# An adaLN block with attention and feed-forward, forward and backward: how the first head group is placed, who normalises, and where chunk 0's side work stands

## The chip, the cores and the metric

The kernel runs on one core of a Trainium2 chip. The metric is device time in microseconds (us), less is better. Five engines work beside each other, each through its own instructions in order: PE (matmul), DVE (VectorE), ACT (ScalarE), POOL (GpSimd) and SP, which here only issues DMAs.

## The reference, cut to what matters

The output is the block's forward value and, through `jax.vjp`, the gradients of nine inputs. Only the forward matters below; the gradients need w_mod, wqkv, w1, w2 and wo transposed too.

```python
mod = (_silu(c) @ w_mod).reshape(c.shape[0], 6, 1, -1)
sa, ca, ga, sb, cb, gb = ...
h = _layernorm(x, axis=-1) * (1 + ca) + sa
# S = 2048 tokens, D = 512, H = 32 heads of Dh = 16
q, k, v = (h @ wqkv) in heads
p = _softmax(einsum('bhqd,bhkd->bhqk', q, k) * Dh ** (-0.5))
x = x + ga * (einsum('bhqk,bhkd->bhqd', p, v) @ wo)
h = _layernorm(x, axis=-1) * (1 + cb) + sb
x = x + gb * ((relu(h @ w1 + b1) ** 2) @ w2 + b2)
```

## The kernel before

**Stages.** `prep` (L824) normalises all tokens, transposes them to h1T, projects the keys of heads 0 to 7 for all tokens and the queries of the first 512, and finds a bound for the scores. Then the forward loop (L1113) runs over 512 units: 4 query chunks of 512 tokens, 8 head groups of 4 heads, 16 key tiles of 128. A unit computes scores for four heads (`fscore`, L544), exponentiates them on ACT in two instructions (L555), and multiplies the values for the unit two before (`fpv`, L557). After a chunk its dense work (projection, feed-forward and their gradients) runs in the next chunk's units. The attention's backward comes last; the change does not touch it.

**The bound.** Instead of a row maximum the softmax subtracts -|q| max|k|. It is carried inside the score matmul: each head's 32 rows of `kts` and `qts` hold 16 rows of keys or queries, one row of ones against one row of the bound, and unused rows. In `prep`, head group 0's rows are put there by small DMAs from the projected tile (`key_rows`, L867, sixteen of them; four for the queries; one for the bound at the end). The other groups are loaded by `fload` (L537) from DRAM, nine DMAs each: four for keys, four for queries, one for the bound (`m_st`). It is issued six units before the group's first unit, into the one of two buffers that is free.

**Order of prep.** For each quarter g of the tokens: statistics on DVE (`stats_tiles`), square root on ACT (`stats_root`), normalisation (`normed1`, L756: two tiles on POOL, two on DVE), PE transposes (`turn1`, L765), four ACT instructions that scale and shift (L775), key projection, its evacuation by ACT (L906). `keep_warm` issues matmuls whose result is not used. At the end come key maxima (L786), square root (L926), the bound row and the first four value tiles.

**Chunk 0's side work.** While units 0 to 127 run, three lists are worked off. `plan_tasks` (L943) puts one task into most units: value tiles, key and query projections for the other heads (`key_tile`, `query_tile`), norms (`key_norm`), bounds (`query_bound`, a DVE chain spread over units), rows of the modulation (`mod_rows`), and PE transposes of queries and keys into token order (`token_tile`). All of them share one PSUM buffer (`pm`, one bank). `later_stage` (L652) runs one stage every fourth unit, at u % 4 = 2: weights and values transposed by DMA into DRAM scratch (stages 4 to 13 and 0 to 3), w_mod transposed (26 to 31: four DMA transposes and a store each), and the normalised tokens recomputed and stored (14 to 25; L692 to L694 are their DVE work). `turn_weights` (L702) transposes w1, w2 and wo by DMA at u % 4 = 0.

**Queues.** Inside `manual_schedule` each engine keeps the written order. Every DMA through `sp` (L173) and `load_rows` (L138) is on SP's queue: a DMA that has to wait for its source holds back all DMAs behind it. `later(lag, ...)` emits an instruction `lag` units later.

## Time and profile before

| what | value |
|---|---|
| runs | median of 13: 2607.01 us, 2602.54 to 2622.65 us |
| the profiled execution | 2605.89 us, of which the span is 2604.1 us |
| busy over the span | PE 90%, ACT 88%, DVE 69%, POOL 14% |
| prep, to the first score matmul | 0 to 48.65 us |
| chunk 0, first exponential to first of chunk 1 | 49.1 to 315.7 us |
| two exponentials of one unit, where nothing stalls | 1.81 us |
| chunks 1 to 3 | 315.7 to about 1065 us |
| attention backward and the end | the rest |

Times in rows of the profile are microseconds from the start of the span. A row of the timeline gives start, duration, engine, line, operation, `output<-input`, shapes, and in square brackets how long the engine had been idle and what ended that. `PEclk` is the share of full clock that PE was granted. SPq stands for DMAs being issued on SP.

### The profile page before, as it was taken

To read this page: it belongs to the slowest core of one execution; us is meant where nothing else is said; L and a number is where in the kernel's file an instruction comes from. 1 tells how busy PE (TensorE), PEld (TensorE's weight loads), DVE (VectorE), ACT (ScalarE), POOL (GpSimd) and SP (SyncE) were. 2 spreads that over 40 slices of the span, in tenths; PEclk is the share of its full clock that TensorE was granted. 3 is DMA by queue.
4 is the path that set the end of the run, shared out by engine and by line. 5 is a ranking of instruction groups with operands and counts; after the bars stand their busy time and mean duration, and the time that the engine had idled before them with its cause. 6 is when DMAs were issued, how large, how long until landed. Compare 5 with 4: busy or idle time off the path is not lost.

```text
span 2604.1 us, 49454 instructions
## 1 busy us (share of the span) xinstructions
PE 2351.6 (90%) x18444; PEld 760.7 (29%) x18444; DVE 1808.6 (69%) x2301; ACT 2303.5 (88%) x3565; POOL 363.6 (14%) x371
## 2 busy tenths in 40 slices
PE   7995989988988889898999999999999999999999
PEld 3232123222322222342222222222232222222343
DVE  5551354445344534578999999999998999999862
ACT  5995999999999999737999999999999999999942
POOL 4000010211233123201110101111011110110100
PEclk8885569997989899999999999999999999999999
DMA  3556565346847673989999999999999999999982
GB/s 128 156 152 169 169 142 135 99 124 136 140 88 139 135 136 77 237 250 195 199 190 199 197 200 193 190 203 197 195 199 198 205 191 197 190 198 206 197 249 73
DMA packets 1227775, 447.49 MB, mean 172 GB/s; under 512 B 1103419, under 2 KB 1198399, under 8 KB 1227278
## 3 DMA queue, kind: packets, MB, share of 16 engines
q1 hardware_dynamic: 1199614, 409.47, 79.8%
q0 software_dynamic: 10944, 16.78, 4.5%
q10 hardware_dynamic: 16976, 18.07, 2.5%
q8 instruction: 145, 2.38, 0.4%
q14 instruction: 96, 0.79, 0.1%
HBM read 96.75 MB, written 73.95 MB: 66 GB/s over the span
## 4 chain that ended last, share of the span: by engine, by line
PE 47%; ACT 34%; DVE 7%; issue 6%; DMA 3%; SPq 2%; POOL 1%; ACTq 0%; DVEq 0%; POOLq 0%
ACT E_u L1552 21%; ACT ET L555 9%; PE dqacc L1624 6%; PE psST L553 5%; PE psS_A L1546 4%; ACT dsT L1695 3%; PE accVK L1597 3%; PE pm L228 3%; PE oacc L569 3%; PE psS_C L1546 2%; PE psS_B L1546 2%; PE pm L393 2%; PE accVK L1606 2%; PE pdh L1810 2%; PE pwq L1844 2%
## 5 line engine op out<-in xcount | busy, mean ns | idle before, releaser
L1566 DVE TENSOR_TENSOR dS_u<-psD_u,E_u 128x1024 bf16<-128x1024 f32 x1024 | 1186.5, 1216 | 99.7 <-PE psS_B L1546 41.0
L555 ACT ACTIVATE ET<-psST 128x1024 bf16<-128x1024 f32 x1024 | 946.3, 1180 | 72.6 <-PE psST L553 72.0
L1552 ACT ACTIVATE E_u<-psS_A 128x512 bf16<-128x512 f32 x768 | 508.8, 663 | 20.0 <-PE psD_u L1564 9.0
L1552 ACT ACTIVATE E_u<-psS_B 128x512 bf16<-128x512 f32 x768 | 504.5, 657 | 3.9 <-PE psS_A L1546 0.5
L1564 PE MATMUL psD_u<-iv,ido 32*128 32x512 bf16 x2048 | 423.0, 397 | 0.2
L553 PE MATMUL psST<-qt_sb,kt_sb 32*128 32x512 bf16 x2048 | 356.9, 439 | 64.8 <-ACT ET L555 33.8
L1552 ACT ACTIVATE E_u<-psS_C 128x512 bf16<-128x512 f32 x512 | 335.0, 654 | 2.3 <-DMA dsT<-dS_u 1.8
L1546 PE MATMUL psS_B<-ik,iq 32*128 32x512 bf16 x768 | 305.4, 398 | 10.3 <-ACT E_u L1552 2.8
L1546 PE MATMUL psS_A<-ik,iq 32*128 32x512 bf16 x768 | 303.3, 395 | 12.5 <-ACT E_u L1552 1.3
L569 PE MATMUL oacc<-ET,vaug 128*32 128x512 bf16 x2048 | 235.1, 449 | 5.7 <-DVE ostage L573 5.7
L1597 PE MATMUL accVK<-dS_u,qz 128*32 128x512 bf16 x2048 | 226.1, 411 | 0.3 <-DVE dS_u L1566 0.2
L1546 PE MATMUL psS_C<-ik,iq 32*128 32x512 bf16 x512 | 194.0, 379 | 33.8 <-ACT dsT L1695 29.8
L1546 PEld LDWEIGHTS <-iq 32*128 32x128 bf16 x2048 | 128.3, 91 | 308.7 <-issue 293.5
L1606 PE MATMUL accVK<-E_u,dOs_tok 128*16 128x512 bf16 x2048 | 209.1, 398 | 0.0
L1642 POOL TENSOR_TENSOR dQacc<-dQacc,dqtmp 128x512 f32<-128x512 f32 x64 | 81.2, 1268 | 870.3 <-ACT dqtmp L1637 870.3
L1624 PE MATMUL dqacc<-dsT,KS_tok 128*32 128x512 bf16 x2048 | 181.1, 462 | 15.1 <-DMA dsT<-dS_u 4.2
L553 PEld LDWEIGHTS <-kt_sb 32*128 32x128 bf16 x2048 | 86.6, 93 | 357.6 <-issue 322.2
L246 DVE COPY part<-pm 128x512 f32<-128x512 f32 (+2 forms) x103 | 63.5, 616 | 132.2 <-PE pm L228 130.3
L1695 ACT ACTIVATE dsT<-ptT 128x1024 bf16<-128x1024 bf16 x128 | 149.0, 1164 | 3.0 <-PE ptT L1587 3.0
L1564 PEld LDWEIGHTS <-ido 32*128 32x128 bf16 x2048 | 106.8, 91 | 106.2 <-issue 100.8
L1597 PEld LDWEIGHTS <-qz 128*32 128x32 bf16 x2048 | 61.0, 98 | 241.2 <-issue 228.0
L1587 PE MATMUL ptT<-identb,dS_u 128*128 128x128 bf16 x1024 | 79.8, 222 | 32.9 <-ACT dsT L1695 26.0
(389 smaller groups left out, 2315.3 us busy)
## 6 DMA issues: line engine op xcount, KB each, us to landing
p_st<-part POOLq DMA_DIRECT2D x36, 256.0 KB, 5.3
kt_sb<-qkT_st SPq DMA_DIRECT2D x124, 64.0 KB
wA<-in_B_w_dram SPq DMA_DIRECT2D x28, 256.0 KB
dsT<-dS_u SPq DMA_TRANSPOSE x448
wB<-w1T_st SPq DMA_DIRECT2D x21, 256.0 KB
wA<-w2T_st SPq DMA_DIRECT2D x21, 256.0 KB
wB<-in_B_w_dram SPq DMA_DIRECT2D x21, 256.0 KB
p_st<-part POOLq DMA_DIRECT2D x25, 192.0 KB, 4.4
```

Source lines behind the costliest of these rows:

```text
L553: PE.matmul(ps[:, hi, :], kt_sb[r:r + 32, kt * P:(kt + 1) * P], qt_sb[r:r + 32, :], start=True, stop=True, tile_position=(r, 0))
L555: ACT.activation(ET[:, 2 * pair:2 * pair + 2, :], ps[:], AF.Exp, scale=SCALE)
L569: PE.matmul(oacc[32 * hq:32 * hq + 32, :], lhsT, ET[:, hq, :], start=(kt == 0), stop=(kt == TT - 1), tile_position=(0, 32 * hq), skip_grou ...
L1546: PE.matmul(psS[:], st["q"][r:r + 32, qt * P:(qt + 1) * P], st["k"][r:r + 32, kc * 512:kc * 512 + 512], start=True, stop=True, tile_positi ...
L1552: ACT.activation(bst[u][0][:, hq, :], sst.pop((u, hq))[:], AF.Exp, scale=SCALE)
L1564: PE.matmul(psD[:, hi, :], st["do"][r:r + 32, qt * P:(qt + 1) * P], st["v"][r:r + 32, kc * 512:kc * 512 + 512], start=True, stop=True, til ...
L1566: DVE.tensor_tensor(dS_u[:, 2 * pair:2 * pair + 2, :], psD[:], E_u[:, 2 * pair:2 * pair + 2, :], ALU.mult)
L1597: PE.matmul(cur["vk"][32 * hq:32 * hq + 32, :], hst[hg]["qz"][:, qt, hq, :], bst[u][1][:, hq, :], start=(qt == 0), stop=False, tile_positi ...
L1606: PE.matmul(acc[32 * hq:32 * hq + DH, :], dOs_tok[:, qt, (hg * 4 + hq) * DH:(hg * 4 + hq + 1) * DH], E_u[:, hq, :], start=False, stop=(qt ...
L1624: PE.matmul(acc[32 * hq:32 * hq + 32, :], KS_tok[:, kc * 4 + kt, h * DH:h * DH + 32], tT[:, :, hq * 4 + kt, :], start=(kt == 0), stop=(kt ...
L1642: POOL.tensor_tensor(dst2, dst, tmp[:], ALU.add)
L1695: ACT.activation(dst, pt[:], AF.Identity)
```

## The change

It has five parts. (1) Head group 0's keys, queries and bounds are no longer moved by DMA. The weight columns of four heads are copied into zero-padded tiles (`wkp`, `wqp`: 32 columns for a head, 16 of them filled), a second product with these lands the keys at their 32-row places, and ACT writes them into `kts[0]`, adding the row of ones as a bias (`onecol`). The norms of these heads are summed by a selector `sel0` that lands them in the bound's row and its neighbour, and one DVE instruction over 128 rows writes query rows and bound row into `qts[0]`. (2) `normed1` uses DVE and ACT, two tiles each, not POOL, and group 0 is normalised before the modulation columns are computed. (3) Four of the six w_mod turns (16 DMA transposes, 4 stores) are issued in `prep`, ahead of the loop; stages 26 to 29 leave the loop, the stages behind them come 16 units earlier, and `turn_weights` 4 units later. (4) Chunk 0's tasks are interleaved: projections alternate with norms or transposes. The norms of keys 0 to 7 are computed once more in units 43 to 49. (5) `mod_rows` and the loads of w_mod's second half move from units 23 to 31 to units 51 to 58.

```diff
@@ -723,9 +723,13 @@
         sbcT = small[:, 0:512].rearrange("p (i q) -> p i q", i=DC)
         sel = small[:, 512:640].rearrange("p (b h) -> p b h", b=4)
         siluc_col, c_col = small[:, 640:644], small[:, 644:648]
-        smallf = small[:, 704:1024].bitcast(F32)
+        smallf = small[:, 704:884].bitcast(F32)
+        nb1 = racc[:, 4, 0:TT]
         sig_col, mv, sd, sel8 = smallf[:, 0:4], smallf[:, 4:36].rearrange("p (t k) -> p t k", k=2), smallf[:, 36:52], smallf[:, 52:60]
         kmx, kmax, epsc = smallf[0:H, 64:80], smallf[0:H, 80:81], smallf[:, 81:82]
+        onecol, kmx0, kmax0 = smallf[:, 82:83], smallf[:, 84:88], smallf[:, 88:89]
+        sel0 = small[:, 888:1016]
+        wkp, wqp = (small[:, i:i + 512].rearrange("p (i h c) -> p i h c", i=DC, h=4) for i in (1024, 1536))
         wmod_v = w_mod.rearrange("(ic p) j -> p ic j", p=P)
         wqkv_v = A_wqkv.rearrange("(ic p) j -> p ic j", p=P)
         xcs, xns, h1Ts, KTs = {}, {}, {}, {}
@@ -757,10 +761,14 @@
             gs = slice(4 * g, 4 * g + 4)
             DVE.reciprocal(rstd1[:, gs], sd[:, gs])
             xns[g] = xn = cb.tile([P, 4, D], BF, name="xnP", tag=("a_c", "xn2_c")[g % 2])
-            for ti in (1, 3, 0, 2):
+            gs1 = slice(4 * g, 4 * g + 4)
+            DVE.scalar_tensor_tensor(out=nb1[:, gs1], in0=mv[:, gs1, 0], scalar=-1.0, in1=rstd1[:, gs1], op0=ALU.mult, op1=ALU.mult)
+            for ti in range(4):
                 t = 4 * g + ti
-                (POOL, DVE)[ti % 2 == 0].tensor_scalar(xn[:, ti, :], xcs[g][:, ti, :], mean1[:, t:t + 1], rstd1[:, t:t + 1],
-                                                       ALU.subtract, ALU.mult)
+                if ti % 2:
+                    ACT.activation(xn[:, ti, :], xcs[g][:, ti, :], AF.Identity, bias=nb1[:, t:t + 1], scale=rstd1[:, t:t + 1])
+                else:
+                    DVE.tensor_scalar(xn[:, ti, :], xcs[g][:, ti, :], mv[:, t, 0:1], rstd1[:, t:t + 1], ALU.subtract, ALU.mult)
 
         def turn1(g):
             h1Ts[g] = h1T = (sP[:, 0:4, :] if g == 3 else cb.tile([P, DC, 512], BF, name="h1T", tag=htags[g])[:])
@@ -847,11 +855,17 @@
             ACT.activation(tiny0[:], onesf[:, 0:1], AF.Sqrt)
             DVE.memset(epsc, EPS)
             DVE.memset(kmx, 0.0)
-            DVE.memset(kts[0][:], 1.0)
-            DVE.memset(qts[0][:], 0.0)
             DVE.tensor_reduce(sel8, identb.rearrange("p (i d) -> p i d", d=DH), AX.X, ALU.add)
             DVE.tensor_tensor(siluc_col, c_col, sig_col, ALU.mult)
             DVE.tensor_copy(sbcT, siluc_col.unsqueeze(2).to_broadcast([P, DC, P]))
+            DVE.tensor_reduce(onecol, identb.rearrange("p (h c) -> p c h", c=32)[:, DH, :], AX.X, ALU.add)
+            POOL.memset(sel0, 0.0)
+            POOL.memset(wkp, 0.0)
+            POOL.memset(wqp, 0.0)
+            for k in range(2):
+                POOL.tensor_copy(sel0.rearrange("p (h c) -> p c h", c=32)[:, DH + k, :], sel8[:, 4 * k:4 * k + 4])
+            POOL.tensor_copy(wkp[:, :, :, 0:DH], wqkv[:, :, D:D + 4 * DH].rearrange("p i (h d) -> p i h d", h=4))
+            POOL.tensor_copy(wqp[:, :, :, 0:DH], wqkv[:, :, 0:4 * DH].rearrange("p i (h d) -> p i h d", h=4))
             POOL.memset(sel, 0.0)
             for b in range(4):
                 POOL.tensor_copy(sel[:, b, 8 * b:8 * b + 8], sel8)
@@ -864,34 +878,48 @@
                 for _ in range(k):
                     PE.matmul(warm[:], ones_bf[:], identb.unsqueeze(1).to_broadcast([P, 4, P]), start=True, stop=True)
 
-            def key_rows(g):
-                for h in range(4):
-                    sp(kts[0][32 * h:32 * h + DH, chunk_cols(g)], KTs[0][DH * h:DH * h + DH, chunk_cols(g)])
-
             def acc4():
                 return psp["p"].tile([P, 512], F32, name="pk", tag="pk", bufs=3)
 
             sq = tmpT[:, 8:13, :]
             pns = {}
 
-            def norms(i, b=0):
-                pns[i] = psp["p"].tile([P, 512], F32, name="pn", tag="pn", bufs=1) if i < 4 else \
-                    psp["p"].tile([P, 512], F32, name="pnq", tag="pcol", bufs=1)
-                head_norms(pns[i], sq[:, i, :], b)
-
+            def norms(i):
+                pns[i] = psp["p"].tile([P, 512], F32, name="pn", tag="pn" if i < 4 else "pcol", bufs=1)
+                PE.matmul(pns[i][:], sel0, sq[:, i, :], start=True, stop=True)
+
+            def widest(g):
+                DVE.tensor_reduce(kmx0[:, g:g + 1], pns[g][:], AX.X, ALU.max)
+
+            def padded_proj(acc, w, g):
+                for ic in range(DC):
+                    PE.matmul(acc, w[:, ic].rearrange("p h c -> p (h c)"), h1Ts[g][:, ic, :], start=(ic == 0), stop=(ic == DC - 1))
+
+            def wmod_turn(j):
+                for q in range(4):
+                    sp(tmpT[:, 4 * (j % 2) + q, :], w_mod[:, (4 * j + q) * P:(4 * j + q + 1) * P], True)
+                if j > 0:
+                    wmod_store(j - 1)
+
+            def wmod_store(j):
+                sp(wmT_st[j], tmpT[:, 4 * (j % 2):4 * (j % 2) + 4, :])
+
+            for j in range(4):
+                wmod_turn(j)
+            wmod_store(3)
             stats_tiles(0, range(4))
             stats_root(0)
             keep_warm(16)
+            stats_tiles(1, (0,))
+            normed1(0)
             mod_cols_of(psp["p"].tile([P, 8], F32, name="pcol", tag="pcol", bufs=1), 0, 2)
             keep_warm(4)
-            normed1(0)
-            stats_tiles(1, (0,))
             for g in range(QC):
                 if g < 3:
                     stats_tiles(g + 1, (1, 2, 3))
                 turn1(g)
                 if g > 1:
-                    key_max(pns[g - 2], 0, g - 2)
+                    widest(g - 2)
                 if g < 2:
                     stats_tiles(g + 2, (0,))
                 if g < 3:
@@ -904,31 +932,35 @@
                 pk = acc4()
                 turned_proj(pk[:], 1, g, 0)
                 ACT.activation(KTs[0][:, chunk_cols(g)], pk[:], AF.Identity)
-                key_rows(g)
+                pk = acc4()
+                padded_proj(pk[:], wkp, g)
+                ACT.activation(kts[0][:, chunk_cols(g)], pk[:], AF.Identity, bias=onecol)
                 if g > 0:
                     norms(g - 1)
-                if g == 2:
+                if g == 1:
                     pq = acc4()
                     turned_proj(pq[:], 0, 0, 0)
                     ACT.activation(sP[:, 4, :], pq[:], AF.Identity)
-                    for h in range(4):
-                        sp(qts[0][32 * h:32 * h + DH, :], sP[DH * h:DH * h + DH, 4, :])
+                if g == 2:
                     square(sq[:, 4, :], sP[:, 4, :])
                     norms(4)
             sp(qkT_st[1, 0:P, :], KTs[0][:])
             sp(qkT_st[0, 0:P, 0:512], sP[:, 4, :])
-            key_max(pns[2], 0, 2)
+            widest(2)
             square(sq[:, 3, :], KTs[0][:, chunk_cols(3)])
             norms(3)
-            key_max(pns[3], 0, 3)
-            DVE.tensor_reduce(kmax, kmx, AX.X, ALU.max)
+            pq = acc4()
+            padded_proj(pq[:], wqp, 0)
+            widest(3)
+            DVE.tensor_reduce(kmax0, kmx0, AX.X, ALU.max)
             qn = cb.tile([P, 512], F32, name="qn", tag="part", bufs=4)
-            ACT.activation(qn[0:H, :], pns[4][0:H, :], AF.Sqrt, scale=kmax)
+            ACT.activation(qn[:], pns[4][:], AF.Sqrt, scale=kmax0)
             ACT.activation(tiny0[:], onesf[:, 0:1], AF.Exp)
-            mrow = sP[0:H, 13, :]
-            DVE.tensor_scalar(mrow, qn[0:H, :], -1.0, None, ALU.mult)
-            sp(qts[0].rearrange("(h c) n -> c h n", h=4)[DH], mrow[0:4, :])
-            sp(m_st[0:8, 0:512], mrow[0:8, :])
+            DVE.scalar_tensor_tensor(out=qts[0][:], in0=qn[:], scalar=-1.0, in1=pq[:], op0=ALU.mult, op1=ALU.add)
+            mrow = sP[:, 13, :]
+            DVE.tensor_scalar(mrow, qn[:], -1.0, None, ALU.mult)
+            for k in range(2):
+                sp(m_st[4 * k:4 * k + 4, 0:512], mrow.rearrange("(h c) n -> c h n", h=4)[DH + k])
             for t in range(4):
                 value_tile(t, acc4()[:])
             POOL.memset(kts[1][:], 1.0)
@@ -982,8 +1014,7 @@
                     head_norms(pn, T["q"][:, hb, :], hb, hb == hbs[0], hb == hbs[-1])
                 for k in "vyt":
                     R[k] = cb.tile([P, 512], F32, name="rt" + k, tag="part", bufs=4)[0:H, :]
-                if hbs[0] != 0:
-                    DVE.tensor_reduce(kmax, kmx, AX.X, ALU.max)
+                DVE.tensor_reduce(kmax, kmx, AX.X, ALU.max)
                 DVE.tensor_scalar(R["v"], pn[0:H, :], kmax, 1e-30, ALU.mult, ALU.max)
 
             def bound(g, hbs):
@@ -1036,35 +1067,37 @@
 
             for t in range(4, TT):
                 at(t - 4, lambda t=t: value_tile(t, mm()[:]))
+            for b, units in ((1, (12, 13, 15, 17)), (2, (23, 24, 26, 28)), (3, (32, 35, 37, 39))):
+                for g, u in enumerate(units):
+                    at(u, key_tile, b, g)
+            for b, units in ((0, (43, 45, 47, 49)), (1, (14, 16, 18, 20)), (2, (25, 27, 29, 31)), (3, (34, 36, 38, 40))):
+                for g, u in enumerate(units):
+                    if b == 0:
+                        at(u - 1, lambda g=g: square(T["k"][:, g, :], KTs[0][:, chunk_cols(g)]))
+                    at(u, key_norm, b, g)
+            for hb, u in ((1, 19), (2, 30), (3, 33)):
+                at(u, query_tile, 0, hb)
             for g in range(QC):
-                at(12 + g, key_tile, 1, g)
-                at(17 + g, key_norm, 1, g)
-                at(26 + g, key_tile, 2, g)
-                at(31 + g, key_norm, 2, g)
-                at(35 + g, key_tile, 3, g)
-                at(40 + g, key_norm, 3, g)
-                at(45 + g, query_tile, 1, g)
-                at(49 + g, token_tile, 0, 0, g)
-                at(54 + g, query_tile, 2, g)
-                at(58 + g, token_tile, 0, 1, g)
-                at(63 + g, query_tile, 3, g)
-                at(72 + g, token_tile, 0, 2, g)
-                at(76 + g, token_tile, 0, 3, g)
+                at(42 + 2 * g, query_tile, 1, g)
+                at(58 + 2 * g, query_tile, 2, g)
+                at(73 + 2 * g, query_tile, 3, g)
+                at(52 + 2 * g - (g == 3), token_tile, 0, 0, g)
+                at(59 + 2 * g, token_tile, 0, 1, g)
+                at((69, 71, 74, 76)[g], token_tile, 0, 2, g)
+                at(81 + g, token_tile, 0, 3, g)
                 for ti in range(4):
-                    at(80 + 4 * g + ti, token_tile, 1, g, ti)
-            for hb, u in ((1, 16), (2, 30), (3, 39)):
-                at(u, query_tile, 0, hb)
+                    at(85 + 4 * g + ti, token_tile, 1, g, ti)
             query_bound(21, 0, (1,), 2)
             at(22, b1_turn)
+            query_bound(41, 0, (2, 3), 1)
+            query_bound(50, 1, (0, 1, 2, 3), 1)
+            query_bound(66, 2, (0, 1, 2, 3), 1)
+            query_bound(80, 3, (0, 1, 2, 3), 1)
             for j in range(3):
-                at(23 + j, mod_rows, j)
-                at(27 + 2 * j, lambda j=j + 3: sp(wmod_slice(j), wmod_v[:, :, j * D:(j + 1) * D]))
-                at(68 + j, mod_rows, j + 3)
+                at(51 + 2 * j, mod_rows, j)
+                at(56 + j, lambda j=j + 3: sp(wmod_slice(j), wmod_v[:, :, j * D:(j + 1) * D]))
+                at(68 + 2 * j, mod_rows, j + 3)
             at(67, lambda: mod_cols_of(mm(), 3, 2))
-            query_bound(44, 0, (2, 3), 1)
-            query_bound(53, 1, (0, 1, 2, 3), 1)
-            query_bound(62, 2, (0, 1, 2, 3), 1)
-            query_bound(71, 3, (0, 1, 2, 3), 1)
 
         NF = len(funits)
 
@@ -1101,7 +1134,7 @@
             with tc.manual_schedule(engines={PE.engine, ACT.engine, DVE.engine, SP.engine, POOL.engine}):
                 prep()
         plan_tasks()
-        stages = [*range(4, 14), *range(4), *range(26, 32), *range(14, 26)]
+        stages = [*range(4, 14), *range(4), 30, 31, *range(14, 26)]
         with ExitStack() as ph2:
             pools["s"] = ph2.enter_context(tc.tile_pool(name="psS", bufs=3, space=bass.MemoryType.PSUM))
             pools["o"] = ph2.enter_context(tc.tile_pool(name="psO", bufs=1, space=bass.MemoryType.PSUM))
@@ -1117,10 +1150,10 @@
                         fscore(u)
                     if 2 <= u:
                         fpv(u - 2)
-                    if u % 4 == 2 and u // 4 < 32:
+                    if u % 4 == 2 and u // 4 < len(stages):
                         later_stage(stages[u // 4])
-                    if u % 4 == 0 and 17 <= u // 4 < 31:
-                        turn_weights(u // 4 - 17)
+                    if u % 4 == 0 and 18 <= u // 4 < 32:
+                        turn_weights(u // 4 - 18)
                     for f, args in plan.pop(u, ()):
                         f(*args)
                     if u < NF - 4:
```

## The prediction

> **What bounds it now.** First the busy time by stretches, since the change touches only prep and chunk 0.
>
> ```profile
> core 0: us, PE busy (x) PEld busy (x) DVE busy (x) ACT busy (x) POOL busy (x), PEclk, DMA share, GB/s
> 0.00:49.00 49.00, 33.66 (x178) 14.81 (x179) 28.94 (x75) 20.63 (x33) 27.46 (x33) 0.83 0.41 133
> 49.00:171.00 122.00, 113.00 (x713) 33.97 (x710) 66.24 (x121) 116.56 (x127) 5.54 (x9) 0.87 0.54 151
> 171.00:199.00 28.00, 26.23 (x212) 9.73 (x210) 16.53 (x33) 28.00 (x32) 0.61 (x1) 0.86 0.60 157
> 199.00:258.00 59.00, 31.65 (x214) 11.48 (x212) 8.24 (x19) 32.82 (x37) 0.61 (x1) 0.50 0.61 153
> 258.00:316.00 58.00, 53.77 (x256) 10.03 (x252) 23.40 (x28) 58.00 (x65) 1.46 (x2) 0.50 0.67 201
> ```
>
> In prep no engine is full: it is a chain. In chunk 0 ACT is the bound wherever nothing stalls (28.00 of 28.00, 58.00 of 58.00): 128 units of 1.815 us are 232.3 us, and chunk 0 takes 266.6 (49.1 to 315.7). So 34.3 us are stalls, and the waits in that stretch say the same:
>
> ```profile
> ACT ET L555 <- PE psST L553: 34.4, 12, 8.8
> PE psST L553 <- DMA qt_sb<-m_st: 17.3, 2, 9.1
> DVE tokP L1028 <- DMA k_st<-tokP: 7.8, 1, 7.8
> DVE tokP L1028 <- DMA q_st<-tokP: 6.7, 1, 6.7
> ```
>
> Taking the starts of the exponentials unit by unit from the timeline, the excess stands at unit 79 (9.2 us), 89 (4.6), 93 (5.5), 95 (8.0), together 27.3, and at 21 to 24, 35, 45, 62 (7.3). The first four are SP's queue: at 79 and 95 the scores wait for a head group's last load, at 89 and 93 the token tiles wait for a store that frees their buffer. SP in that place:
>
> ```profile
> 196.67 5.44 SPq L173 DMA_TRANSPOSE tmpT<-in_w_mod_dram  x4
> 203.72 0.34 SPq L173 DMA_DIRECT2D wmT_st<-tmpT  x1
> 204.16 2.13 SPq L138 DMA_DIRECT2D kt_sb<-qkT_st  x4
> 206.34 1.80 SPq L138 DMA_DIRECT2D qt_sb<-qkT_st  x4
> 208.18 0.56 SPq L138 DMA_DIRECT2D qt_sb<-m_st  x1
> 210.05 0.71 PE L553 MATMUL psST<-qt_sb,kt_sb 32*128 32x512 bf16 x4 [9.11 <-DMA qt_sb<-m_st]
> ```
>
> The reader is to see: a DMA transpose holds SP 1.3 us, a load 0.46; the store waits for its transposes, and the nine loads stand behind it.
>
> **Part 3, w_mod turns out of the loop.** SP's account for units 58 to 95 (38 units, 69.0 us). Before: 24 w_mod transposes, 14 of w1, 2 of the output, 40 x 1.3 = 52.0; 8 small row DMAs x 0.63 = 5.0; three head loads x 4.3 = 12.9; some 18 others x 0.5 = 9.0; waits of wmT stores 6 x 1.5 = 9.0. Sum 87.9, so 18.9 over. After: 16 transposes go (-20.8), 4 stores and their waits (-8.0): 59.1, which fits. Order matters too, so I follow the queue. Group 5's loads (unit 74) have only x loads, row DMAs and one output transpose ahead of them and land some 4 us before unit 80; the token stores stand at least 4 units ahead of their reuse. Units 79, 89 and 93 lose their 19.3 us. Group 6: from unit 80 SP has 12 w1 transposes (15.6), row DMAs and output transpose (3.8), five stores (2.5), then nine loads (4.2), landing about 2 us later: 28.1 us against the 29.0 to unit 96. Groups of four w1 transposes took 5.2 to 6.9 us in this trace, so 2 us may be missing: I put 2.0 in place of 8.0 (ends 0 and 8).
>
> New: in units 56 and 57 two w_mod loads of 512 KB are issued just before group 4's loads (unit 58). In the trace of before they followed head loads, so no row prices the order; its loads there were slow already (6.9 us to issue), but no wait at unit 64 shows. The Trainium skill (DMA: Bandwidth & Descriptors, "Queues, rings and completion order") says each DMA engine consumes its ring in order, so 1 MB stands ahead of them: at the 350 GB/s that the opening loads reach (2 to 18 us) 3.0 us. By the row 0, by the rule 3.0; I take 1.5. Net of part 3 in the loop: -27.3 + 2.0 + 1.5 = **-23.8**.
>
> In prep the 16 transposes stand behind all input loads and ahead of nothing that the first scores need, since part 1 takes SP out of that chain. Eight from 13 us to 23.4, then store, wait of 2, four, twice over: SP is free at about 42 to 48 us. The DMA engines moved almost nothing from 19 to 44 us, so they have room. Next in the queue with a date is group 1's load at unit 10 (about 62 us): 14 us of cover. Gone, each us shows at unit 16.
>
> **Parts 1 and 2, prep.**
>
> ```profile
> 11.87 4.28 POOL L762 TENSOR_SCALAR xnP<-xP,mean,rstd 128x512 bf16<-128x512 bf16 x2 [2.83 <-issue]
> 16.95 1.44 ACT L775 ACTIVATE h1T<-ptP,modcol 128x512 bf16<-128x512 bf16 x2 [7.84 <-PE ptP L772]
> 48.65 0.40 PE L553 MATMUL psST<-qt_sb,kt_sb 32*128 32x512 bf16 x4 [1.81 <-DVE vP L801]
> ```
>
> Before, POOL's two tiles (2.14 each) end at 16.15 and ACT's h1T starts at 16.95. After, DVE's pair (0.53 each) and ACT's pair are done by about 11.3. No row shows ACT on this form; h1T's 0.72 is nearest, the evacuation's 0.60 the lower end, 0.78 the upper. PE then limits: the modulation columns need w_mod and end at 11.3, four warm matmuls to 13.1, eight transposes to 14.1. Gain 2.85. h1T of the four quarters starts at 16.95, 23.78, 30.90 and 38.09, 21.1 us for three periods. A new period: four h1T and the root 3.2; last key product 0.26 to 0.43; four padded products 1.04 to 1.7; norms 0.4; once the query product 1.04 to 1.7; eight transposes 0.5 to 0.9; ACT's 1.44 of normalising and 0.6 evacuation lie beside PE. Three periods: 18.1 at full PE clock, 21.1 at half. PE is denser than before, so I take 19.3: gain 1.8 more. Tail: from last h1T's start to the first value copy before 7.0 (38.09 to 45.09); after, the keys' evacuation, square, norm, two maxima and root are the same, the DVE instruction into qts adds 0.68: 7.6. The bound's DMA goes, but gains nothing: in the built program the first score waits for the fourth value copy on DVE (PSUM handed over), as the row above shows, 3.5 us after the first. Gain 2.85 + 1.8 - 0.6 = **-4.0** (ends -1 and -6). The 20 row DMAs and POOL's vaug and padding work were on no chain; costs 0.
>
> **Parts 4 and 5.** The other 7.3 us are PE's clock:
>
> ```profile
> 109.20:112.60 3.40, 2.35 (x22) 0.68 (x18) 1.96 (x3) 3.40 (x5) 0.61 (x1) 1.00 1.29 245
> 112.60:116.00 3.40, 3.40 (x17) 0.68 (x17) 0.68 (x1) 3.40 (x5) 0.00 (x0) 0.50 0.84 256
> 116.00:119.40 3.40, 3.40 (x15) 0.76 (x13) 1.12 (x2) 2.48 (x3) 0.00 (x0) 0.50 0.12 23
> ```
>
> After a stretch of norms alone (PE busy 2.35 of 3.40) the clock is 0.50, the next projection takes 1.89 instead of 1.04, and the unit 3.1 us. The Trainium skill (TensorE: Matmul & The Clock Gate, "Why this matters for your kernels") asks only for no idle gap over some 3 us; by that rule PE, never idle so long here, would not slow, and interleaving is worth 0. By the rows stretches at 69 to 73% go cold and those with a projection in them (80% up) stay at 1.00. Alternating units have 2.9 busy of 3.63, 80%. Trace over rule: they stay warm, except where light units still meet: 20 to 22 (1.9 x 0.8), 40 and 41 (1.9 x 0.4), 56 and 57 (1.2 x 0.3), 2.7 in all. Net **-4.6**.
>
> Against it: the DVE work of three later_stage steps (four of 0.33 and two of 1.26, 3.9 us) now falls at units 82, 90, 94 among token tiles, whose copies free the one pm bank; before it fell after them. A copy comes about 1.1 us late, PE is some 0.6 ahead: 0.5 each, 1.5. Units 42 to 49 carry copies, squares, maxima and bound steps of 1.8 us of DVE in 1.815: 0.5. **+2.0** (ends 0 and 7).
>
> **Sum.** -4.0 - 23.8 - 4.6 + 2.0 = -30.4. From the profiled 2605.9 (1.8 outside its span, unchanged): 2575.5. That execution lies 1.1 below the median, so runs should have 2576.6.
>
> **Rivals.** (a) *Loads late again*: group 4 behind the w_mod loads loses 5 us, group 6 the old 8.0; 9.5 over my 3.5: 2586. For: SP at 97% from unit 80. Against: 28.8 us less on SP overall. 0.18. (b) *Prep gains little, DVE blocks token tiles*: -1 in place of -4.0, and 2.2 for each of three collisions in place of 0.5: +8: 2585. For: the value copies on DVE still end the chain, PE may be at half clock. 0.12. (c) *Slower*: interleaving keeps PE at half clock. Then each of 36 heavy units (12 key, 15 query tiles, 6 mod rows, 3 bounds) costs 3.1 - 1.83 = 1.27, 45.7, against 7.3 + 27.3 + 4.0 won: +7.1, 2614. It decides from 31 of 36 cold. Against: a cold heavy unit fills PE, and the full stretches at 112.6 and 116.0 were followed by 1.00. 0.05. (d) *w_mod turns aren't ahead*: if a transpose needs 2.2 us or more beside the loads, SP comes to the loop late by more than the 14 us, and groups 1 and 2 stall instead: about 2590 to 2605. 0.03. Mine: 0.62.
>
> **Range.** Best: all 34.4 of stalls and 6 of prep, 2566; worst of (a) or (b) with some of the other 2592; some 2 us of noise: 2565 to 2595. This kernel's measurement tells about 0.2% (5.2 us): faster by more 0.90, within 0.04, slower 0.06.
>
> **What shows it.** First score near 44.6 us, waiting for the fourth value copy; no POOL in prep's chain. No wait for m_st's load near unit 80, under 3 us at 64 and 96. PEclk 1.00 over units 25 to 80 but for two or three short stretches. Chunk 0 near 241 us, chunks 1 to 3 and the backward as before within 3 us. Wrong would be: many units of 3.1 us (c), or PE idle ahead of units 64 and 96 (a).

## The result, and the profile after

The changed kernel takes **2582.45 us** (median of 11 runs, 2578.91 to 2590.18) against 2608.3 us (48 runs, 2597.39 to 2622.65): ratio 0.990, 95% interval 0.9884 to 0.9915. Its profiled execution took 2576.21 us, of which the span is 2574.3 us. The forecast was 2576.6 us, range 2565 to 2595. Run again later (`e8_after_again` below), the same kernel took 2577.4 us, ratio 0.9885 (0.9855 to 0.9916). The profiled execution is faster than any of the 11 runs; why the median lies above it is taken up with the sum below.

Where the time went, from the two traces (first exponential, first exponential of chunk 1, last of the forward, first and last of the backward):

| us | start | chunk 0 | chunks 1 to 3 | gap | backward | end | span |
|---|---|---|---|---|---|---|---|
| before | 49.1 | 266.5 | 748.4 | 120.5 | 1283.2 | 136.4 | 2604.1 |
| after | 43.2 | 240.4 | 750.2 | 120.6 | 1286.5 | 133.4 | 2574.3 |
| difference | -5.9 | -26.1 | +1.8 | +0.1 | +3.3 | -3.0 | -29.8 |

Busy time by stretches, for the changed kernel:

```profile
core 0: us, PE busy (x) PEld busy (x) DVE busy (x) ACT busy (x) POOL busy (x), PEclk, DMA share, GB/s
0.00:43.00 43.00, 32.89 (x197) 15.24 (x197) 28.03 (x79) 28.19 (x45) 10.86 (x30) 0.96 0.80 202
43.00:165.00 122.00, 109.55 (x730) 33.50 (x727) 69.61 (x129) 120.09 (x131) 6.78 (x11) 0.97 0.57 160
165.00:193.00 28.00, 24.96 (x206) 8.96 (x204) 13.38 (x29) 28.00 (x32) 0.61 (x1) 1.00 0.76 209
193.00:226.00 33.00, 26.72 (x188) 9.74 (x186) 21.88 (x41) 29.01 (x33) 0.61 (x1) 0.58 0.61 144
226.00:284.00 58.00, 54.30 (x276) 11.74 (x272) 13.61 (x15) 58.00 (x65) 1.23 (x2) 0.50 0.63 187
```

In prep POOL fell from 27.46 to 10.86 us of work and ACT rose from 20.63 to 28.19: the normalisation moved. PE's clock there is 0.96, before 0.83. In chunk 0, ACT was busy 32.82 of 59 us over units 79 to 95 before; the fourth row, units 81 to 95, now has 29.01 of 33. Units 79 to 95 took 58.0 us and take 36.0. The waits of chunk 0 (43 to 284 us):

```profile
ACT ET L555 <- PE psST L553: 9.2, 8, 3.5
...
PE ptk L1056 <- DVE tokP L1059: 3.1, 2, 1.5
...
PE ptk L1056 <- DVE tokP L1064: 2.3, 1, 2.3
PE psST L553 <- DVE vP L809: 1.8, 1, 1.8
```

Columns: total us, times, longest. ACT's waits fell from 34.4 to 9.2 us; the loads (`qt_sb<-m_st`, 17.3 before) and the stores that held the token buffers are gone from the list. In their place stands DVE's copy of a token tile, 5.4 us in three waits. One of them, at unit 83, as the timeline shows it:

```profile
194.51 0.41 DVE L1064 COPY tokP<-ptk 128x512 bf16<-128x512 bf16 x1
...
195.47 1.36 DVE L692 TENSOR_SCALAR tmpT<-tmpT,mean,rstd 128x512 bf16<-128x512 bf16 x4
...
196.87 1.23 DVE L693 TENSOR_TENSOR tmpT<-tmpT,modbc 128x2048 bf16<-128x2048 bf16 x1
...
198.13 1.22 DVE L694 TENSOR_TENSOR tmpT<-tmpT,modbc 128x2048 bf16<-128x2048 bf16 x1
199.27 0.42 DVE L1064 COPY tokP<-ptk 128x512 bf16<-128x512 bf16 x1
...
199.74 0.58 PE L1056 MATMUL ptk<-identb,sP 128*128 128x128 bf16 x4 [2.28 <-DVE tokP L1064]
```

The three lines of `later_stage` stand ahead of the copy on DVE for 3.9 us; PE's next transposes wait 2.28 us for it, the scores stand behind them on PE, and the unit takes 4.0 us in place of 1.8. Group 5's loads, 9.2 us late before, now land in time:

```profile
183.98 2.59 SPq L138 DMA_DIRECT2D qt_sb<-qkT_st  x4
186.61 0.54 SPq L138 DMA_DIRECT2D qt_sb<-m_st  x1
```

The last is issued at 186.6 us and unit 80's first exponential starts at 191.5.

The start of the loop:

```profile
10.22 0.73 DVE L771 TENSOR_SCALAR xnP<-xP,small,rstd 128x512 bf16<-128x512 bf16 x2
10.34 1.52 ACT L769 ACTIVATE xnP<-xP,racc,rstd 128x512 bf16<-128x512 bf16 x2 [0.76 <-DVE racc L765]
...
13.95 1.45 ACT L783 ACTIVATE h1T<-ptP,modcol 128x512 bf16<-128x512 bf16 x2 [2.09 <-PE ptP L780]
...
42.70 0.10 PEld L553 LDWEIGHTS <-kt_sb 32*128 32x128 bf16 x4 [2.25 <-DVE vP L809]
```

h1T starts at 13.95 (before 16.95), and the first score waits for the fourth value copy, as before.

### The profile page after: what moved, and what is told of

It reads as the page before. It is cut to its first block, busy times and chain, and to the rows that moved or that the text cites. A ratio compares the mean times of both kernels' runs of the same rounds, so it can differ in the third digit from the quotient of the medians.

```text
span 2574.3 us, 49491 instructions
## 1 busy us (share of the span) xinstructions
PE 2339.3 (91%) x18468; PEld 759.5 (30%) x18468; DVE 1811.9 (70%) x2316; ACT 2310.7 (90%) x3577; POOL 347.4 (13%) x370
## 3 DMA queue, kind: packets, MB, share of 16 engines
q8 instruction: 145, 2.38, 0.4%
## 4 chain that ended last, share of the span: by engine, by line
PE 47%; ACT 35%; DVE 7%; issue 6%; DMA 2%; SPq 1%; ACTq 0%; POOL 0%; DVEq 0%; POOLq 0%
ACT E_u L1585 21%; ACT ET L555 9%; PE dqacc L1657 6%; PE psST L553 5%; PE psS_A L1579 4%; PE accVK L1630 3%; ACT dsT L1728 3%; PE oacc L569 3%; PE pm L228 3%; PE psS_C L1579 3%; PE psS_B L1579 2%; PE accVK L1639 2%; PE pm L393 2%; PE pdh L1843 2%; PE pwq L1877 2%
## 5 line engine op out<-in xcount | busy, mean ns | idle before, releaser
L553 PE MATMUL psST<-qt_sb,kt_sb 32*128 32x512 bf16 x2048 | 353.4, 430 | 56.3 <-ACT ET L555 43.3
L1579 PE MATMUL psS_B<-ik,iq 32*128 32x512 bf16 x768 | 306.3, 399 | 11.8 <-ACT E_u L1585 4.5
L569 PE MATMUL oacc<-ET,vaug 128*32 128x512 bf16 x2048 | 229.9, 439 | 6.8 <-DVE ostage L573 6.8
## 6 DMA issues: line engine op xcount, KB each, us to landing
p_st<-part POOLq DMA_DIRECT2D x25, 192.0 KB, 4.4
```

The lines of the kernel that those rows point to most:

```text
L553: PE.matmul(ps[:, hi, :], kt_sb[r:r + 32, kt * P:(kt + 1) * P], qt_sb[r:r + 32, :], start=True, stop=True, tile_position=(r, 0))
L569: PE.matmul(oacc[32 * hq:32 * hq + 32, :], lhsT, ET[:, hq, :], start=(kt == 0), stop=(kt == TT - 1), tile_position=(0, 32 * hq), skip_grou ...
L1579: PE.matmul(psS[:], st["q"][r:r + 32, qt * P:(qt + 1) * P], st["k"][r:r + 32, kc * 512:kc * 512 + 512], start=True, stop=True, tile_positi ...
```

## The experiments

All profiles in one table (us; "half clock" is the time at which PE was granted half its clock from the forward's last exponential to the end of the execution, so over gap, backward and end; 8 to 14 us of each figure lie outside the backward):

| kernel | start | chunk 0 | start + chunk 0 | backward | half clock |
|---|---|---|---|---|---|
| before | 49.1 | 266.5 | 315.6 | 1283.2 | 172.4 |
| after | 43.2 | 240.4 | 283.6 | 1286.5 | 176.6 |
| e1_turns_alone | 61.0 | 244.8 | 305.8 | 1289.9 | 183.2 |
| e2_turns_in_loop | 42.8 | 264.6 | 307.4 | 1300.9 | 216.5 |
| e3_blocks | 41.7 | 248.8 | 290.5 | 1290.3 | 183.2 |
| e4_h1_later | 42.6 | 237.2 | 279.8 | 1302.0 | 219.5 |
| e5_pool_norm | 58.2 | 240.7 | 298.9 | 1288.4 | 186.4 |
| e6_norm_alone | 41.8 | 264.1 | 305.9 | 1287.3 | 195.1 |
| e7_stalls_out | 41.9 | 239.2 | 281.1 | 1292.1 | 192.0 |
| e8_after_again | 41.2 | 244.3 | 285.5 | 1283.3 | 165.3 |
| e9_turns_apart | 42.6 | 236.0 | 278.6 | 1297.0 | 216.8 |
| e10_apart_alone | 43.3 | 240.4 | 283.7 | 1286.9 | 178.7 |
| e11_e4_again | 43.3 | 236.6 | 279.9 | 1287.4 | 180.2 |
| e12_e2_again | 42.5 | 263.8 | 306.3 | 1292.0 | 189.7 |

### e1: the w_mod turns ahead, nothing else

```diff
 # before, with wmod_turn and wmod_store as in the change, and
...
+            for j in range(4):
+                wmod_turn(j)
+            wmod_store(3)
             stats_tiles(0, range(4))
...
-        stages = [*range(4, 14), *range(4), *range(26, 32), *range(14, 26)]
+        stages = [*range(4, 14), *range(4), 30, 31, *range(14, 26)]
...
-                    if u % 4 == 0 and 17 <= u // 4 < 31:
-                        turn_weights(u // 4 - 17)
+                    if u % 4 == 0 and 18 <= u // 4 < 32:
+                        turn_weights(u // 4 - 18)
```

> The kernel before with only the w_mod turns moved ahead (stages and turn_weights as in the changed kernel); head group 0 still goes through SP's row DMAs. My account (SP's queue is what holds chunk 0, and part 1 is what lets the turns go ahead): the 16 transposes hold SP to about 43 us, the 20 row DMAs and the bound row follow, so the first score comes near 57 us instead of 48.65 (+8 or more), while chunk 0 shrinks from 266.6 to about 243 us as the waits at units 79, 89, 93, 95 go. Together about -14 us, near 2592. Rival (chunk 0's stalls come from the order of the tasks, not from the w_mod turns): chunk 0 stays within 5 us of 266 and the whole gets slower by 8.

Measured: 2600.32 us, ratio 0.9962 (0.9947 to 0.9977). Chunk 0 fell by 21.7 us, so the turns' place, not the order of the tasks, is the large part of chunk 0's gain. But the loop starts 11.9 us later than before (I had expected 8 or more), and the total gained 8.7 us where I had expected 14. SP in the timeline of this kernel:

```profile
41.92 1.76 SPq L173 DMA_DIRECT2D wmT_st<-tmpT  x2
43.77 7.67 SPq L173 DMA_DIRECT2D kt_sb<-KT  x12
...
60.28 0.62 PE L553 MATMUL psST<-qt_sb,kt_sb 32*128 32x512 bf16 x4 [13.38 <-DMA rows_st<-racc]
```

The key rows' DMAs come out of the queue only when the turns are through, at 43.8 us, and the first score waits 13.4 us for the queue. Without these rows on SP, as in the changed kernel, the turns hold up no first score. So part 1 is what makes part 3 free. That is read from this wait: no run has parts 2 and 3 without part 1, and none has part 1 alone.

### e2: the changed kernel with the turns back in the loop

```diff
 # after, with
-            for j in range(4):
-                wmod_turn(j)
-            wmod_store(3)
...
-        stages = [*range(4, 14), *range(4), 30, 31, *range(14, 26)]
+        stages = [*range(4, 14), *range(4), *range(26, 32), *range(14, 26)]
...
-                    if u % 4 == 0 and 18 <= u // 4 < 32:
-                        turn_weights(u // 4 - 18)
+                    if u % 4 == 0 and 17 <= u // 4 < 31:
+                        turn_weights(u // 4 - 17)
```

> The changed kernel with part 3 alone undone: all six w_mod turns in the loop, stages and turn_weights where they were. My account: first score stays at 42.7 us, and waits of scores for a head group's loads or of token tiles for a store come back in units 64 to 100; chunk 0 goes from 240.3 to about 258 us (252 to 267). Rival (interleaving has spread SP's work enough): chunk 0 stays under 246 us.

Measured: 2611.8 us, ratio 1.0006 (0.9991 to 1.0021): without part 3 no gain of the whole change can be measured in the time. Chunk 0 takes 264.6 us (263.8 the second time), 24.2 more than after. The waits of its chunk 0:

```profile
ACT ET L555 <- PE psST L553: 33.1, 10, 11.3
...
PE psST L553 <- DMA qt_sb<-m_st: 14.0, 2, 8.8
DVE tokP L1056 <- DMA q_st<-tokP: 13.8, 1, 13.8
PE ptk L1053 <- DVE tokP L1056: 13.5, 2, 11.6
```

The old waits are back: two late head loads (14.0 us), and token copies that stand behind a store (DVE waits 13.8 us for `q_st` ahead of them). With e1 this settles the main account: SP's queue was the bound at units 79 to 95. In the trace e2 still reaches chunk 1 8.2 us earlier than before (307.4 against 315.6), but the median of its ten runs doesn't show it; the last section comes back to this.

### e3: the tasks in blocks

```diff
 # after, plan_tasks with
-            for b, units in ((1, (12, 13, 15, 17)), (2, (23, 24, 26, 28)), (3, (32, 35, 37, 39))):
+            for b, units in ((1, (12, 13, 14, 15)), (2, (23, 24, 25, 26)), (3, (32, 33, 34, 35))):
...
-                at(42 + 2 * g, query_tile, 1, g)
-                at(58 + 2 * g, query_tile, 2, g)
-                at(73 + 2 * g, query_tile, 3, g)
+                at(42 + g, query_tile, 1, g)
+                at(58 + g, query_tile, 2, g)
+                at(75 + g, query_tile, 3, g)
 # norms, token tiles and mod_rows in blocks likewise
```

> The changed kernel with the same chunk 0 tasks in blocks (projections in a row, then norms or transposes in a row) in nearly the same units. My account: after each block of norms or transposes the granted clock falls to 0.50 and the next projection unit takes 3.1 us; 3 to 5 such places, chunk 0 longer by 4 to 8 us. Rival (order is of no consequence, the clock falls only with idle gaps): within 1 us of 240.3.

Measured: 2588.9 us, ratio 0.9919 (0.9897 to 0.9941). Chunk 0 is 8.4 us longer than after's, but 2.8 us of it stand at units 5 and 6, where no task was moved (e8 to e10 explain them). So 5.6 us are the blocks': new stalls of 1.1 to 1.4 us at units 40, 66 and 68 and of 0.7 at 59 and 75, where fuller units follow norms or transposes alone (unit 58 stalls in after too). At unit 40, which starts at 119.3 us:

```profile
114.00:117.40 3.40, 2.35 (x22) 0.62 (x17) 1.36 (x2) 3.40 (x5) 0.00 (x0) 1.00 0.65 240
117.40:120.80 3.40, 3.40 (x17) 0.71 (x16) 0.68 (x1) 3.40 (x5) 0.00 (x0) 0.50 0.46 118
```

After the stretch of norms PE is at half clock (0.50), and the unit takes 3.2 us. Interleaving is worth about what the clock term of the forecast gave it (4.6). Part 5 was not tried alone.

### e4: the h1 stages behind the token tiles

```diff
 # after, with
-        stages = [*range(4, 14), *range(4), 30, 31, *range(14, 26)]
+        stages = [*range(4, 14), *range(4), 30, 31, 14, 15, 16, *[17] * 6, 18, 20, 21, 22, 23, 24, 25]
```

Stage 17 does nothing; it keeps the places in between.

> The changed kernel with the three stages that recompute normalised tokens on DVE moved from units 82, 90, 94 to 102, 106, 110 (the fourth from 106 to 122), behind the token tiles. My account: the stalls at units 83 (2.2 us), 91 (1.5) and 95 (1.4) are this DVE work ahead of the token tile's copy and go: chunk 0 240.3 to about 235.2, total -5 us. Rival (the one at 95 is head group 6's load, due at unit 96 behind w1's transposes): 83 and 91 go, 95 stays, -3.7 us.

Measured: 2580.69 us, ratio 0.9885 (0.9861 to 0.991). The stalls at units 83 (2.2 us) and 91 (1.5) are gone: those two were DVE's. The stall at unit 95 stayed at 1.4 us, as the rival had it, and under the DVE wait another came to light:

```profile
219.34 0.55 SPq L138 DMA_DIRECT2D qt_sb<-m_st  x1
...
221.19 0.71 PE L553 MATMUL psST<-qt_sb,kt_sb 32*128 32x512 bf16 x4 [1.28 <-DMA qt_sb<-m_st]
```

Group 6's last load is issued at 219.3 us and lands some 1.3 us late. In after's trace the same unit names DVE. Two waits of like length lay over each other, and the list named one.

### e5 and e6: what normalising on DVE and ACT is worth

```diff
 # e5: after, with (e6: before, with the reverse, and group 0 ahead of the modulation columns)
...
-                if ti % 2:
-                    ACT.activation(xn[:, ti, :], xcs[g][:, ti, :], AF.Identity, bias=nb1[:, t:t + 1], scale=rstd1[:, t:t + 1])
-                else:
-                    DVE.tensor_scalar(xn[:, ti, :], xcs[g][:, ti, :], mv[:, t, 0:1], rstd1[:, t:t + 1], ALU.subtract, ALU.mult)
+                (POOL, DVE)[ti % 2 == 0].tensor_scalar(xn[:, ti, :], xcs[g][:, ti, :], mean1[:, t:t + 1], rstd1[:, t:t + 1],
+                                                       ALU.subtract, ALU.mult)
```

> After with part 2 undone: the four normalising instructions of a prep quarter are back on GpSimd and VectorE, everything else as in after. My account: what part 2 buys isn't the 2.14 us against 1.5 us of one tile but a queue. In after's trace GpSimd has the padding copies (behind the Q columns of wqkv, about 16.4 us) and the fills of vaug until about 20.4 us ahead of anything new, so its first pair ends near 24.7, the first h1T starts near 25.5 in place of 13.95, the quarters' periods go back to about 7 us (after: 5.3 to 5.9), and the first score's exponential starts at 54 to 58 us (after: 43.2). Chunk 0 itself stays at 240 to 243 us. Rival: who normalises makes little difference once part 1 has taken SyncE and the row DMAs out of the chain; then the first exponential is at 43 to 46 us.

> Before with part 2 alone: VectorE and ScalarE normalise in prep, in after's order; the key rows and the bound still go through DRAM and SyncE, and the w_mod turns stay in the loop. My account: nearly all that prep won (5.9 us in the profiles) is part 2's, since the first score waits for the fourth value copy in both kernels and the row DMAs were on no chain; then the first exponential starts at 43 to 45.5 us (before 49.1, after 43.2) and chunk 0 stays at 264 to 268 us. Rival: with h1T early the rows' and the bound's way through DRAM end the chain instead, the first score waits for a DMA, and the first exponential starts at 46.5 us or later.

Measured, one execution each: e5 2593.72 us, e6 2597.82 us, beside 2607.25 us of the kernel before. e5's loop starts at 58.2 us, 15.0 later than after's and 9.1 later than before's. POOL in e5's timeline:

```profile
15.87 0.40 POOL L864 COPY small<-wqkv_nat 128x256 bf16<-128x256 bf16 x1 [2.60 <-DMA wqkv_nat<-in_A_wqkv_dram]
...
17.38 2.33 POOL L869 MEMSET vaug<- 128x528 bf16 x1
19.32 0.39 POOL L757 COPY mean<-small 128x4 f32<-128x4 f32 x1
19.84 4.28 POOL L766 TENSOR_SCALAR xnP<-xP,mean,rstd 128x512 bf16<-128x512 bf16 x2
```

The padding copies of part 1 wait for wqkv's loads and stand, with the fills of `vaug` behind them, ahead of the normalisation: it starts at 19.84 us, 8 us after before's 11.87. e6 starts at 41.8 us, 7.3 earlier than before and no later than after, with the rows still going through SP:

```profile
41.24 0.13 PEld L553 LDWEIGHTS <-kt_sb 32*128 32x128 bf16 x4 [2.27 <-DMA rows_st<-racc]
41.27 0.40 PE L553 MATMUL psST<-qt_sb,kt_sb 32*128 32x512 bf16 x4 [1.81 <-DVE vP L806]
```

Its score is released by the value copy on DVE, with a DMA behind the weight load's wait at practically the same moment. So all that prep won is part 2's. Part 1 costs prep nothing only because part 2 is there (e5), and part 3 only because part 1 is (e1). e6's start was earlier than I expected (43 to 45.5): its first h1T is early (13.30 us, below), and from there to the first exponential it takes 28.5 us where after takes 29.2.

### e7: three edits against the stalls at once

```diff
 # e4, with
-            for b, units in ((1, (12, 13, 15, 17)), (2, (23, 24, 26, 28)), (3, (32, 35, 37, 39))):
+            for b, units in ((1, (12, 13, 15, 17)), (2, (22, 24, 26, 28)), (3, (32, 35, 37, 39))):
...
-            at(22, b1_turn)
+            at(23, b1_turn)
...
-                        if funits[u][2] == (10 if u < 7 * TT else 4) and u + TT < NF:
+                        if funits[u][2] == (10 if u < 4 * TT else 4) and u + TT < NF:
```

> After with the h1 stages behind the token tiles (as in e4_h1_later), the loads of head groups 5 to 7 issued six units earlier (at unit 4 of the group before, as group 7's already is), and one key tile and one bound step exchanged at units 22 and 23, so that no two light units meet there. My account: the stall at unit 95 (1.4 us) was group 6's load, and the 0.9 to 1.4 us at unit 23 the half clock after two light units: both go, chunk 0 takes 234 to 236 us (e4 237.2, after 240.4), and the time is 4 to 7 us below after's but for the backward's own scatter. Rival for unit 95: issued earlier, the loads push w1's transposes and the token stores back on SyncE, and a token tile waits for its buffer near units 84 to 95: 1.5 us or more there. Rival for unit 23: the light units merely meet somewhere else, and a 2.3 to 3.2 us unit stands between 20 and 28 all the same.

Measured: 2580.07 us, ratio 0.9888 (0.9863 to 0.9912); chunk 0 is 239.2 us, not 234 to 236. Unit 95 takes 1.8 us: it was the load, and no token tile waits in its place. Units 22 and 24 now take 3.2 us each, 2.7 us of stall against 2.3 around there in e4, so the rival held for the clock:

```profile
81.20:84.60 3.40, 2.38 (x18) 0.55 (x13) 1.93 (x4) 3.40 (x6) 0.00 (x0) 0.95 0.15 31
84.60:88.00 3.40, 3.40 (x21) 0.83 (x20) 0.82 (x2) 2.52 (x4) 0.00 (x0) 0.55 0.62 173
```

A stretch with PE busy 2.38 of 3.40 is followed by one at half clock; two light units had only been put elsewhere. And 2.9 us came in at units 5 and 6, which the next three runs are about.

### e8 to e10: the queue behind the turns

e8 is the changed kernel, unaltered. e9 is e4 with the earlier loads of e7 and four buffers for the turns; e10 is after with the four buffers alone:

```diff
 # the definitions of wmod_turn and wmod_store go too
...
-            for j in range(4):
-                wmod_turn(j)
-            wmod_store(3)
+            wmod_bufs = [tmpT[:, 0:4, :], tmpT[:, 4:8, :], sP[:, 5:9, :], sP[:, 9:12, :], tmpT[:, 13:14, :]]
+            for j, buf in enumerate(wmod_bufs):
+                for q in range(buf.shape[1]):
+                    k = 4 * j + q - (j == 4)
+                    sp(buf[:, q, :], w_mod[:, k * P:(k + 1) * P], True)
+            for j in range(3):
+                sp(wmT_st[j], wmod_bufs[j])
+            sp(wmT_st[3][:, 0:3, :], wmod_bufs[3])
+            sp(wmT_st[3][:, 3:4, :], wmod_bufs[4])
```

> The changed kernel once more, unaltered, beside e7 on the same chip. First question: does the backward, which the change doesn't touch, differ between executions of one program? If its length is an execution's own (1283 to 1302 us over five profiles, with 172 to 219 us of it at half PE clock), it comes out other than 1286.5 us by several us, and up to the first backward exponential the times agree with the first profile within 2 us. Rival: it belongs to the program; then it is 1286.5 within 1.5 us with 175 to 178 us of half clock.

> e4_h1_later with two edits: the loads of head groups 5 to 7 six units earlier (as in e7_stalls_out), and the four w_mod turns of prep in four buffers of their own (eight slots of tmpT, seven of sP and one more of tmpT) in place of two shared ones, so that the transposes don't wait for stores and the stores stand behind all of them. My account of the stall at units 5 and 6 (0 to 3.5 us in the executions of the kernels with turns in prep): SyncE comes out of the turns at 43.0 to 44.2 us in all of them, whatever prep does, since each half of tmpT waits some 2.9 us for its store; eight small stores stand between that and the first v_st store (47.5 to 48.6 us), which frees the value tiles' buffer. With own buffers SyncE is free at 36 to 39 us, v_st is issued at 42 to 44 us, and units 5 and 6 take 1.8 us each in every execution; start plus chunk 0 is 277 to 279 us (after 283.6, its second profile 285.5, e4 279.8, e7 281.1). Rival: the stall comes from the way of the v_st store itself, beside other transfers, and it stays at 1 us or more with v_st issued early.

> After with the four buffers of the w_mod turns alone. If my account holds, units 5 and 6 don't stall and the start plus chunk 0 is 281 to 282.5 us (41.5 plus 240), with the stalls at 83, 91 and 95 as in after; the prediction's cover of 14 us behind the turns was then none, since the first v_st store and not group 1's load is the next of the queue with a date. Rival: as for e9_turns_apart.

Measured: e8 2577.4 us, ratio 0.9885 (0.9855 to 0.9916); e9 2582.76 us, 0.9894 (0.9871 to 0.9917); e10 2584.22 us, 0.9909 (0.9884 to 0.9933). e8 starts 2.0 us earlier than the first profile of the same kernel, and loses 3.5 us at units 5 and 6. Its timeline:

```profile
48.64 1.71 SPq L173 DMA_DIRECT2D v_st<-vP  x2
...
52.03 0.69 DVE L809 CAST vP<-pm 128x512 bf16<-128x512 f32 x1 [3.06 <-DMA v_st<-vP]
...
52.77 1.41 PE L804 MATMUL pm<-wqkv_nat,h1T 128*128 128x512 bf16 x4 [2.41 <-DVE vP L809]
```

Value tile 8 needs the buffer of tiles 0 to 3, which its store frees. That store stands on SP behind the turns, whose last store is issued by 43.0 to 43.6 us in all six profiles with parts 1 to 3 in prep and shared buffers, whatever their start, and behind six small DMAs. PE, idle for 2.4 us, then takes 1.41 us for four products that take 1.04 in after, at full clock; from 53.3 us its clock is 0.50. So the loss is more than the wait. e9's SP:

```profile
38.76 1.17 SPq L173 DMA_DIRECT2D wmT_st<-tmpT  x1
...
44.16 5.98 SPq L173 DMA_DIRECT2D v_st<-vP  x2
```

With buffers of their own the turns end at 39.9 us (e10: 40.6), `v_st` is issued at 44.2 (44.7) and not at 47.5 to 48.6, the copy of value tile 8 no longer waits for it, and units 5 and 6 take 1.8 us in both kernels. e9's start plus chunk 0 is 278.6 us, the shortest of all.

e10's, 283.7, is above my 281 to 282.5: its start is 43.3, not 41.5. The start is another thing that belongs to the execution: from the first h1T to the first exponential all ten profiles with parts 1 and 2 in prep take 29.2 us, and the first h1T starts between 12.03 and 14.11 us. Ahead of it PE waits for w_mod's loads (2.4 us in two waits in after, 2.5 in e8); what sets the moment was not followed further.

With the shared buffers an early start only lengthens the wait for the store: the executions that started at 41.2, 41.7 and 41.9 us lost 2.8 to 3.5 us at units 5 and 6, the three that started at 42.6 to 43.3 (after, e4, e11) lost none there, though DVE waited 0.9 and 1.2 us for the store in after and e11. e9 and e10 started at 42.6 and 43.3, so units 5 and 6 need not have stalled there with shared buffers either: what they show is the earlier `v_st` and no wait for it, not a stall taken away.

e9 has chunk 0 and the start 5.0 us shorter than after, and yet its median is not below after's: e9's interval and after's lie over each other. The gain shows in the trace, not in the time.

### e11 and e12: is the backward's length the program's?

> e4_h1_later once more, unaltered. Its first profile had the longest backward of all (1302.0 us, of it 219.5 at half PE clock), though the edit lies in chunk 0. If the backward's length is an execution's own, it comes back here as 1283 to 1298 us, with less time at half clock; chunk 0 is 235 to 241 us again. Rival: moving the h1 stages shifts what the backward meets, and it is 1300 to 1304 us again, with 215 us or more at half clock.

> e2_turns_in_loop once more, unaltered. Its first profile had the second longest backward (1300.9 us, 216.5 at half clock). As an execution's own it is 1283 to 1298 us here; as the program's 1299 to 1303. Chunk 0 is 263 to 267 us again with the loads and stores late at units 79 and 95.

e4 took 1302.0 us in the backward, and unaltered the next time 1287.4, with 39 us less at half clock; e2 1300.9 and 1292.0, 27 us less. So the program alone doesn't fix the length: two profiles of one program differ by up to 14.6 us. These repeats ran on another chip than the first profiles, but the scatter is there on one chip too: e8's six runs of one program take 2572.66 to 2596.34 us, the longest with a granted clock of 0.908, the others 0.917 to 0.920. e8 against after (1283.3 and 1286.5) had left this open. What decides it isn't found.

## Why the prediction was right, and where not

**Part 3, net -23.8.** Right: from after to e2 it is 24.2 us (23.4 by the second profile). The stalls at 79, 89 and 93 went. Of its additions, +1.5 for group 4's load behind the w_mod loads measured 0 (unit 64 has no stall): the 0 of the row was the right cost. That is no case against the ordered rings that the prediction cites from the Trainium skill (DMA: Bandwidth & Descriptors, "Queues, rings and completion order"): the group's last load is issued at 157.77 us and unit 64's scores start at 161.91, so a short delay would not show. Group 6's +2.0 measured 1.4, in e4, where nothing covers it.

**"14 us of cover" behind the turns.** Wrong, and it was my reading of the queue that failed: I took the next load with a date, group 1's at unit 10. A store with a date comes first, `v_st`, whose landing frees the buffer that value tile 8 needs (written at unit 4, felt at unit 5). The cover was about 0: no loss in the first profile, 3.5 us in e8's. That the first profile lost nothing was luck: its start was late (43.2 us).

**Prep, -4.0.** Right in sign, too small: -5.9. Start of h1T 3.0 (forecast 2.85); three periods of 5.31, 5.89 and 5.63 us, gain 4.3 (1.8); tail 1.4 longer (0.6). The mis-sized term is the period: I took 19.3 us for three, between full and half clock; they took 16.8, with PE at full clock from 13.9 us on. The two ends were summed wrongly as well: the terms written there give 17.2 at full clock and 21.6 at half, not 18.1 and 21.1, so the full-clock sum was within 0.4 of what came. "Padding work at 0" was true only beside part 2: in e5, on the chain, it holds the normalisation back to 19.84 us.

**Clock, 7.3 down to 2.7.** Right in mechanism: stalls of 2.0 us at units 23 to 26 and 1.3 at 58 follow the light units 20 to 22 and 56/57 that I had named; 40/41 stayed warm. At unit 58 the windows read as forecast:

```profile
143.70:147.10 3.40, 2.94 (x24) 0.90 (x21) 2.38 (x4) 3.40 (x5) 0.00 (x0) 1.00 0.77 207
147.10:150.50 3.40, 2.47 (x28) 0.99 (x24) 1.43 (x3) 3.40 (x6) 0.00 (x0) 0.99 1.10 272
150.50:153.90 3.40, 3.40 (x17) 0.70 (x18) 0.97 (x2) 2.70 (x4) 0.00 (x0) 0.51 0.94 264
```

The stretch with PE busy 86% is followed by full clock, the one at 73% by half. The latter holds 0.93 us of idle time in all, no gap near 3 us, and still the clock fell: here the measurement goes against the rule that the prediction quotes from the Trainium skill (TensorE: Matmul & The Clock Gate, "Why this matters for your kernels"), and e3's 5.6 us are what light units in a row cost. But the busy share is no threshold either. In e4 a stretch at 60% is followed by full clock:

```profile
91.50:94.90 3.40, 2.03 (x17) 0.59 (x13) 2.23 (x4) 2.69 (x4) 0.00 (x0) 1.00 0.19 60
94.90:98.30 3.40, 3.38 (x24) 1.00 (x24) 2.00 (x5) 3.40 (x5) 0.00 (x0) 1.00 0.20 48
```

And from 198 us on after's PE stays at half clock to the end of chunk 0, though it is busy 54.30 of the 58 us from 226 to 284. In those 58 us ACT is busy all the time and the units take 1.81 us, so the half clock costs nothing there. What the clock goes by is not found here.

**DVE's h1 stages, "0.5 each, 1.5".** The place was right, the size not: units 83 and 91 stall 2.2 and 1.5 us, and e4 takes 3.2 us off chunk 0 (3.8 in its second profile). I set PE's lead against the average lateness of a copy; the copy comes after the whole run of six instructions, 3.9 us, and PE's lead was spent within the first unit. The busy DVE of units 42 to 49 cost 0.3 us, not 0.5.

**The sum.** The misses in chunk 0 cancel: 240.2 forecast, 240.4 measured, with loads that cost less than allowed and DVE and the clock more. That closeness is luck, as is the profile's total: 2575.5 us forecast, 2576.21 taken. The median of its runs lies 6.2 us above that profile. I had set before's profile against before's median and assumed that after's would stand the same way. The scatter undoes that: in after's runs those with a granted clock of 0.916 to 0.919 took 2576.2 to 2580.9 us, those with 0.912 to 0.914 took 2582.5 to 2590.2. That it is the backward's is likely from the profiles, but these runs have no trace of their own. Chunks 1 to 3 came within the 3 us I had allowed, the backward 3.3 above.

**The rivals.** (a) Loads late again: only 1.4 us of it, at unit 95. (b) DVE in the token tiles' way: its mechanism is real at two units, while its other half, prep gaining little, fell. (c) Interleaving keeps PE cold: no; blocks do, by 5.6 us. My reason against it, that a full stretch warms PE again, doesn't hold everywhere: from 198 us on full stretches stay at half. (d) Turns late into the loop: groups 1 and 2 didn't stall; the turns are felt earlier, at the store of unit 5.

## What to carry to other kernels

In an in-order DMA queue look for the next entry with a date, stores that free a buffer included, before you call the room behind a moved block cover. A change's parts can be worth something only together: here one part's helper work is harmless only because another took the normalisation off that engine, and moving the transposes keeps its whole gain only where no first-score row goes through the same queue (e1: 21.7 us won in chunk 0, 11.9 lost before it). When a stall goes, ask whether a second wait of like length stood under it.
